# Loading one piece of a weight by three transfers of 112, 8 and 8 partitions instead of one of 128

## The chip, the cores and the metric

The kernel runs on one core of a Trainium2 chip. The time is that of one launch on the device, in microseconds (us); the figure for a kernel is the median of several runs. A profile is one execution of the same program recorded by the hardware profiler. It tells the time of every instruction, and it tells of the core's 16 DMA engines how many packets and bytes they moved, and when.

## What is computed

One decoding step of a transformer block: attention over a cache of 4,096 keys and values for each of 4 sequences and 32 heads, beside a small network, all in float32.

```python
x = A_x
xn = _layernorm(x, axis=-1)
return x + _A_ref(xn, A_k_cache, A_v_cache, A_wq, A_wo) + _B_ref(xn, B_w1, B_w2, B_w3, B_w4)
```

`_A_ref` is the attention. Its last step is the output projection, a product with the weight `wo` of 4,096 rows and 512 columns (8 MB):

```python
q = (x @ wq).reshape(B, Sq, H, Dh).transpose(0, 2, 1, 3)
scores = jnp.einsum("bhqd,bhkd->bhqk", q, k_cache) * (Dh ** -0.5)
p = _softmax(scores, axis=-1)
o = jnp.einsum("bhqk,bhkd->bhqd", p, v_cache)
return o.transpose(0, 2, 1, 3).reshape(B, Sq, H * Dh) @ wo
```

With one position for each sequence the shifts of `_B_ref` bring in nothing but zeros, so of that network `w3` and `w4` alone are read.

## The kernel before

The two caches are 2 x 256 MB. The kernel walks over 32 groups of four heads of one sequence (`NJ`), and for each group it loads 8 MB of keys into one of two buffers `ks`, and 8 MB of values into the buffer `vs`. VectorE multiplies the keys with the query and sums (lines 329 and 330), ScalarE takes the exponentials (348), TensorE multiplies them with the values (382). All loads are issued from one queue, SP, in the order of the program, each as soon as its buffer is free.

The end of the program is what the change touches. When VectorE has used the last keys (`SUMMED[LAST]`), SP loads `wo` into the buffer `ks` that is then free. Partition p holds 32 rows of `wo` (`WC`), one behind the other, 2 KB each. The loading is cut by rows of each partition, `wo_cuts`: 16, 8, 4, 2 and 1 rows; the last row follows in two halves of 256 columns (lines 290 to 292). Each of the seven pieces has a semaphore of its own, `wo_sems[n]`, that its transfer raises by 16.

TensorE takes the pieces in the same order (lines 414 to 434) and waits before each for its semaphore. It multiplies the rows of the first two pieces into four partial results in the bank `y`, and those of the others into the bank `total`; behind the piece of four rows (24 to 27) it adds the partial results to `total` through ScalarE's copy `ys` and the matrix `sel`. Behind each half of the last row the result is copied out of `total` by VectorE and ScalarE (436, 437) and stored by a DMA of four partitions (441). The four partitions are the four sequences.

Of the kernel before, what the change touches and what calls it, by code (L numbers as in the profile page):

```python
# [44 lines left out]
P = 128  # L45
# [4 lines left out]
PE, DVE, ACT = mybir.EngineType.PE, mybir.EngineType.DVE, mybir.EngineType.Activation  # L50
# [38 lines left out]
def decode_block(ctx: ExitStack, tc: tile.TileContext, x, k, v, wq, wo, w3, w4, out):  # L89
    nc = tc.nc  # L90
# [57 lines left out]
    def blocks4(start, stop, w, m, src):  # L148

        for t in range(4):  # L150
            i = nc.tensor.matmul(total[32 * t:32 * t + m, :], w, src[:, P * t:P * t + P], start=start, stop=stop)  # L151
        return i

    do = Steps(nc)
# [4 lines left out]
    wo_sb = ks[LAST % 2].rearrange("p (c n) -> p c n", c=WC)  # L159
# [125 lines left out]
    do.wait("SP", [SUMMED[LAST]])  # L285
    wo_r = wo.rearrange("(p c) n -> p c n", c=WC)
    for (c0, c1), sem in zip(wo_cuts, wo_sems):
        nc.sync.dma_start(wo_sb[:, c0:c1], wo_r[:, c0:c1]).then_inc(sem, 16)  # L288
    half = D // 2
    for n, sem in enumerate(wo_sems[-2:]):  # L290
        n *= half
# [120 lines left out]
    ys = os.rearrange("p m d -> p (m d)")  # L412
    do.wait("PE", [X_ok])
    for (c0, c1), sem in zip(wo_cuts, wo_sems):
        do.wait("PE", [(sem, 16)])
        for c in range(c0, c1):
            if c < 24:
                t = (c + 2) % 4
                i = nc.tensor.matmul(y[32 * t:32 * t + B, :], X[:, c, :], wo_sb[:, c], start=False, stop=(c >= 20))
            else:  # L420
                i = blocks4(False, False, X[:, c, :], B, wo_sb[:, c])
        d = do("PE", lambda e: i)

        if c1 == 24:
            ys_ok = do("ACT", lambda e: e.copy(ys, y), d)
        elif c1 == 28:
            do.wait("PE", [ys_ok])
            blocks4(False, False, sel, 32, ys)
# [49 lines left out]
```

## Time and profile before

| | us |
|---|---|
| median of 3 runs | 1302.82 |
| lowest and highest run | 1302.47, 1303.36 |
| span of the profiled execution, first to last instruction | 1301.2 |
| TensorE busy | 370.9 |
| VectorE busy | 1164.4 |
| ScalarE busy | 93.6 |

The difference between the median and the span, 1.6 us, lies around the instructions that the profile counts. VectorE is busy for 89% of the span. The share of the DMA engines is in the next section, with the rows that belong to it. A DMA is shown twice: as the instruction of the engine that issues it (SPq, ACTq), which is short, and as the packets that the 16 DMA engines move afterwards; the time "to landing" runs from the issue to the last increment of its semaphore.

### The profile page before, as it was taken

The page shows a single profiled execution, that of the slowest core. Times are in us where ns is not written, and L with a number is a line of the kernel's source. Part 1 is how long each engine was busy: PE and PEld are TensorE (multiplying, and loading weights), DVE is VectorE, ACT ScalarE, POOL GpSimd, SP SyncE. Part 2 cuts the span into 40 slices and gives each one's busy share as a digit, 9 for nine tenths or more (in the row PEclk, how much of TensorE's full clock was granted, in tenths as well). Part 3 has the DMA queues.
Part 4 walks back from the last instruction along what each step waited for, and adds up shares of the span by engine and source line. Part 5 has one row for each costly group of instructions (what it writes and reads, how often), then busy time and mean ns, then how long its engine had stood idle before and what let it go on. Part 6 is the DMA issues. An engine that isn't in the chain of part 4 may idle for free. (4 is left out here: it accounts for less than half of the span.)

```text
span 1301.2 us, 6686 instructions
## 1 busy us (share of the span) xinstructions
PE 370.9 (29%) x2652; PEld 132.4 (10%) x2652; DVE 1164.4 (89%) x323; ACT 93.6 (7%) x332; POOL 2.5 (0%) x14
## 2 busy tenths in 40 slices
PE   3221233321233321233331133332123332123338
PEld 1000111100011110011110011110001110001112
DVE  3499999999999999999999999999999999999990
ACT  1000000000000000000000000000000000000001
POOL 0000000000000000000000000000000000000000
PEclk9655666655666665666665666665666665566668
DMA  9999999999999999999999999999999999999998
GB/s 404 446 422 448 425 441 427 433 435 425 445 423 445 425 443 425 433 435 427 443 423 445 425 443 427 435 433 429 439 423 447 423 443 427 439 429 433 435 423 372
DMA packets 10830, 561.08 MB, mean 431 GB/s; under 512 B 1212, under 2 KB 1476, under 8 KB 1736
## 3 DMA queue, kind: packets, MB, share of 16 engines
q1 hardware_dynamic: 10808, 561.00, 99.7%
q8 instruction: 3, 0.05, 0.0%
q14 instruction: 3, 0.02, 0.0%
q10 hardware_dynamic: 16, 0.01, 0.0%
HBM read 561.00 MB, written 0.01 MB: 431 GB/s over the span
## 5 line engine op out<-in xcount | busy, mean ns | idle before, releaser
L329 DVE TENSOR_TENSOR ks<-ks,qb 128x8192 f32<-128x8192 f32 x64 | 556.3, 8692 | 59.2 <-DVEq L297 54.2
L330 DVE TENSOR_REDUCE sc<-ks 128x64 f32<-128x8192 f32 x64 | 555.9, 8686 | 2.2
L382 PE MATMUL pv<-vs,pw 128*32 128x512 f32 x1984 | 285.6, 740 | 869.7 <-PEq L297 869.7
L382 PEld LDWEIGHTS pv<-vs,pw 128*32 128x32 f32 x1984 | 78.5, 133 | 1052.2 <-issue 1052.2
L353 ACT COPY os<-pv 128x512 f32<-128x512 f32 x32 | 18.8, 586 | 827.7 <-ACTq L297 827.7
L348 ACT ACTIVATE pw<-sc,small 32x128 f32<-32x128 f32 x128 | 50.9, 398 | 275.2 <-ACTq L297 274.0
L387 PE MATMUL poz<-sel,os 128*128 128x4 f32 x256 | 32.8, 252 | 28.0 <-PEq L297 28.0
L387 PEld LDWEIGHTS poz<-sel,os 128*128 128x128 f32 x256 | 31.0, 191 | 56.1 <-issue 56.1
L348 ACT ACTIVATION_READ_ACCUMULATOR pw<-sc,small 32x1 f32 x128 | 23.5, 184 | 0.0
L436 DVE COPY os<-total 4x128 f32<-4x128 f32 x2 | 0.6, 282 | 15.0 <-PE total L434 15.0
L335 DVE TENSOR_REDUCE small<-sc 128x1 f32<-128x128 f32 x32 | 9.2, 286 | 4.7
L363 DVE RECIPROCAL rz<-oz 128x96 f32<-128x96 f32 (+1 forms) x2 | 1.1, 553 | 13.6 <-ACT oz L355 13.5
L389 PE MATMUL poz<-rs,ones 128*128 128x4 f32 x64 | 11.7, 253 | 0.0
L321 DVE STREAM_TRANSPOSE qb<-qg 128x128 f32<-128x128 f32 x32 | 10.0, 311 | 1.1
L264 DVE STREAM_TRANSPOSE vs<-pw 128x1024 f32<-128x1024 f32 x1 | 1.2, 1245 | 10.4 <-ACT pw L263 10.4
L320 DVE COPY qg<-qT 128x4 f32 x32 | 5.4, 170 | 5.1 <-issue 4.7
L389 PEld LDWEIGHTS poz<-rs,ones 128*128 128x128 f32 x64 | 9.7, 192 | 0.0
L382 PE MATMUL pv<-ks,pw 128*32 128x512 f32 x64 | 9.5, 757 | 0.0
L202 DVE TENSOR_REDUCE lns<-vs 4x1 f32<-4x512 f32 x1 | 0.7, 674 | 9.5 <-DMA vs<-in_A_x_dram 9.5
L355 ACT COPY oz<-poz 128x8 f32 x32 | 5.3, 166 | 50.8 <-ACTq L297 50.8
L215 PE MATMUL pt<-vs,pw 4*128 4x4 f32 x16 | 4.0, 372 | 16.4 <-DVE pw L209 16.4
L336 DVE STREAM_TRANSPOSE tr<-small 128x32 f32<-128x32 f32 x32 | 6.8, 212 | 1.1
(75 smaller groups left out, 78.4 us busy)
## 6 DMA issues: line engine op xcount, KB each, us to landing
ks<-in_A_k_cache_dram SPq DMA_DIRECT2D x2, 4096.0 KB, 26.9
vs<-in_B_w_dram SPq DMA_DIRECT2D x2, 3584.0 KB, 14.1
ks<-in_A_wo_dram SPq DMA_DIRECT2D x1, 4096.0 KB, 21.8
ks<-in_A_wo_dram SPq DMA_DIRECT2D x1, 2048.0 KB, 26.3
ks<-in_A_wo_dram SPq DMA_DIRECT2D x1, 1024.0 KB, 28.3
ks<-in_A_wo_dram SPq DMA_DIRECT2D x1, 512.0 KB, 29.1
ks<-in_A_k_cache_dram SPq DMA_DIRECT2D x31, 42.2
vs<-in_A_v_cache_dram SPq DMA_DIRECT2D x31, 26.8
```

The source lines that it names most:

```text
L320: step(e.tensor_copy(qg, pairs[:, s, bass.ds(j, 1)].rearrange("p o n -> p (o n)")))
L321: step(e.transpose(qb.rearrange("p (n m) -> p n m", m=HP), qg.unsqueeze(2).to_broadcast([P, DH // HP, HP])))
L329: step(e.tensor_tensor(out=kt, in0=kt, in1=qb.unsqueeze(1).to_broadcast([P, w, DH]), op=ALU.mult))
L330: step(e.reduce_sum(sc[s][:, c:c + w], kt, axis=AX.X))
L335: step(e.reduce_max(rm, sc[s], axis=AX.X))
L336: step(e.transpose(tr[s], rm.to_broadcast([P, HP])))
L348: i = nc.scalar.activation(pw[hp, :, 4 * h:4 * h + 4], sc[s][hp, :].rearrange("p (g w) -> p g w", w=4), AF.Exp, bias=small[hp, s, 1:2], sc ...
L353: nc.scalar.copy(os, pv.rearrange("p (m d) -> p m d", m=4)).then_inc(sems["copied"], 1)
L355: nc.scalar.copy(ozs[:, s, :, bass.ds(j, 1)].rearrange("p n o h -> p n (o h)"), poz[:, 0:2 * G].rearrange("p (n h) -> p n h", n=2)).then_i ...
L382: i = nc.tensor.matmul(pv[32 * t:32 * t + 32, :], pw[:, g, :], vt[:, 4 * g:4 * g + 4, :], start=(g < 4), stop=(g >= NG - 4))
L387: nc.tensor.matmul(poz[:, 0:G], os[:, m, :], sel.rearrange("p (h m) -> p m h", m=4)[:, m, 0:G], start=(m == 0), stop=(m == 3))
L389: nc.tensor.matmul(poz[:, G:2 * G], ones.to_broadcast([P, P]), rs, start=True, stop=True).then_inc(sems["poz"], 1)
```

## The change

The piece of rows 24 to 27 of each partition (1 MB, 8 KB on each partition) is loaded by three transfers: one for the partitions 0 to 111, one for 112 to 119, one for 120 to 127. All three raise the same semaphore, and TensorE waits for 48 instead of 16. The same bytes go to the same places, and the other six pieces are loaded as before.

```diff
     for (c0, c1), sem in zip(wo_cuts, wo_sems):
-        nc.sync.dma_start(wo_sb[:, c0:c1], wo_r[:, c0:c1]).then_inc(sem, 16)
+        for p0, p1 in ((0, 112), (112, 120), (120, P)) if c0 == 24 else ((0, P),):
+            nc.sync.dma_start(wo_sb[p0:p1, c0:c1], wo_r[p0:p1, c0:c1]).then_inc(sem, 16)
...
     for (c0, c1), sem in zip(wo_cuts, wo_sems):
-        do.wait("PE", [(sem, 16)])
+        do.wait("PE", [(sem, 48 if c0 == 24 else 16)])
```

On SP's queue, at the end of the program, the loads of `wo` (`ks` is the buffer, `in_A_wo_dram` the weight in memory; the numbers are partitions x elements) stood before as follows:

```order
L288 DMA ks<-in_A_wo_dram 128x8192
L288 DMA ks<-in_A_wo_dram 128x4096
L288 DMA ks<-in_A_wo_dram 128x2048
L288 DMA ks<-in_A_wo_dram 128x1024
L288 DMA ks<-in_A_wo_dram 128x512
L292 DMA ks<-in_A_wo_dram 128x256 x2
L441 DMA out_dram<-os 4x256
```

and now, with all line numbers one higher:

```order
L289 DMA ks<-in_A_wo_dram 128x8192
L289 DMA ks<-in_A_wo_dram 128x4096
L289 DMA ks<-in_A_wo_dram 112x2048
L289 DMA ks<-in_A_wo_dram 8x2048 x2
L289 DMA ks<-in_A_wo_dram 128x1024
L289 DMA ks<-in_A_wo_dram 128x512
L293 DMA ks<-in_A_wo_dram 128x256 x2
L442 DMA out_dram<-os 4x256
```

Two issues more stand ahead of the last four pieces, which move back by two places. The instructions of the other engines keep their order and their number.

## The prediction

> **What bounds the kernel now.** I read the head of the page, the DMA part and the table of queues first, then the chain that ended last, then the last 6 us by the timeline and by short windows.
>
> ```profile
> span 1301.2 us, 6686 instructions
> DMA  9999999999999999999999999999999999999998
> DMA packets 10830, 561.08 MB, mean 431 GB/s; under 512 B 1212, under 2 KB 1476, under 8 KB 1736
> q1 hardware_dynamic: 10808, 561.00, 99.7%
> q8 instruction: 3, 0.05, 0.0%
> ```
>
> The 16 DMA engines are busy from the first slice to the last (nines, and 99.7% in SP's queue q1). What decides the time is the bytes and how evenly the engines carry them. One engine moves 561.00 MB / (16 x 0.997 x 1301.2 us) = 27.0 GB/s, so **8 KB take it 0.303 us**, and the piece of 1 MB, eight such rows on each engine, 2.42 us. The chain says the same of the end:
>
> ```profile
> 1268.12 28.33 DMA ks<-in_A_wo_dram
> 1296.45 0.04 issue
> 1296.49 1.27 PE total L151 x40
> 1297.77 0.01 issue
> 1297.78 1.02 PE total L151 x24
> 1298.80 0.70 PE total L434 x8
> 1299.50 0.02 issue
> 1299.52 0.26 ACT os L437
> ```
>
> The DMA in the first row is the piece that the change cuts. It is issued at 1268.12, lies in the queue behind other loads, and lands at 1296.45; TensorE starts on it 0.04 us later. From there the chain looks like TensorE's, but the timeline of its weight loads shows that every later piece is waited for too:
>
> ```profile
> 1297.78 0.33 PEld L151 LDWEIGHTS total<-ks,X 128*4 128x4 f32 x16 [0.28 <-DMA ks<-in_A_wo_dram]
> 1298.39 0.11 PEld L151 LDWEIGHTS total<-ks,X 128*4 128x4 f32 x8 [0.29 <-DMA ks<-in_A_wo_dram]
> 1298.74 0.10 PEld L434 LDWEIGHTS total<-ks,X 128*4 128x4 f32 x4 [0.23 <-DMA ks<-in_A_wo_dram]
> 1299.06 0.10 PEld L434 LDWEIGHTS total<-ks,X 128*4 128x4 f32 x4 [0.23 <-DMA ks<-in_A_wo_dram]
> ```
>
> In brackets stands the idle time ahead of the row and what ended it. The end therefore moves with the landing of the last half row, just before 1299.06, nearly one to one.
>
> A transfer lands when its slowest engine is done. Windows at the end show how unequal the engines are (us, TensorE's granted clock, share of the 16 DMA engines by the packets that start in the window, GB/s):
>
> ```profile
> 1296.80:1297.20 0.40, 1.00 0.94 328
> 1297.20:1297.60 0.40, 1.00 0.60 210
> 1297.60:1297.90 0.30, 1.00 0.33 120
> 1297.90:1298.20 0.30, 1.00 0.27 96
> 1298.20:1298.50 0.30, 1.00 0.21 72
> 1298.50:1298.80 0.30, 1.00 0.04 14
> ```
>
> Nearly all 16 work until about 1297.1; then they run out one by one. From 1297.9 to 1298.2 some four are left (0.27 x 16 = 4.3), after 1298.2 about three (0.21 x 16 = 3.4), and these carry the end, some 1.6 us behind the first. One source of the lateness is in the trace. The three packets of q8 are fetches of instructions; a window around the last of them reads:
>
> ```profile
> DMA packets 5, 0.07 MB, mean 655 GB/s; under 512 B 0, under 2 KB 0, under 8 KB 0
> q1 hardware_dynamic: 4, 0.05, 115.2%
> q8 instruction: 1, 0.02, 67.9%
> ```
>
> 67.9% of 16 engines x 0.1 us (1292.8 to 1292.9) is 1.09 us on one engine, which so falls behind by as much. Nothing makes up for it later, because no engine ever runs empty and each transfer gives all engines the same.
>
> **The change, part by part.** *Two issues more on SP.*
>
> ```profile
> 1267.27 2.50 SPq L288 DMA_DIRECT2D ks<-in_A_wo_dram  x5
> 1269.82 0.90 SPq L292 DMA_DIRECT2D ks<-in_A_wo_dram  x2
> ks<-in_A_wo_dram SPq DMA_DIRECT2D x2, 128.0 KB, 28.8
> ```
>
> An issue takes about 0.45 us (0.90 / 2), so the four pieces behind are issued 0.9 us later, the last ones near 1271.2. They wait some 28.8 us in the queue today; 0.9 of it hides behind the loads ahead of them. Without that cover it would cost 0.9. Nothing else on SP is near: the store follows at 1299.5. Cost 0.
>
> *The wait for 48.* It replaces the wait for 16 in front of the same matmul, so TensorE gets no instruction more. The same matmuls stand behind it (rows 28 to 31 and both halves), and the copies and stores behind those. Cost 0, apart from a later landing.
>
> *The engines' rows.* Here lies the effect. How many engines a transfer uses can be counted from its closing packets: 75 loads of 128 partitions and three transfers of four partitions (x and two stores) make 75 x 16 + 3 x 4 = 1212 packets, exactly the page's "under 512 B 1212" (and q1's 10808 packets are 75 x (128 + 16) and 8 for one store). So 128 partitions close on 16 engines and four partitions on four, one each. The trace has no transfer of 112 or of 8. Bounds for 112: seven rows on each of 16 engines, or eight on each of 14; I take seven, nearer to the 128. Bounds for 8: all rows on one engine, or one on each of eight; I take eight, nearer to the four. Whether both small transfers use the same eight engines the trace doesn't show: if they use different ones, every engine has eight rows as today and nothing changes; if the same, eight engines get 7 + 1 + 1 = 9 rows and eight get 7. The three transfers of four partitions give no engine's name; I take the same, as two equal requests. Then **eight engines end 0.303 us later than today, eight 0.303 us earlier**.
>
> ```profile
> q1 hardware_dynamic: 8, 0.00, 1.0%
> q10 hardware_dynamic: 8, 0.00, 1.0%
> ```
>
> Closing packets add little. In the window 1299.8 to 1301.2, above, the two stores' 16 packets take 2.0% of 16 x 1.4 us, 28 ns each with the data among them, so two more are under 0.06 us. [...]
>
> *Sum.* The last landing is that of the latest engine. If at least one of the last three is among the eight with nine rows, the end moves by +0.303 us; if all four late ones are among the others, by up to -0.303. The trace names no engine. Taken at random, the four all fall into one given half in (8 x 7 x 6 x 5) / (16 x 15 x 14 x 13) = 4% of cases, the last three in (8 x 7 x 6) / (16 x 15 x 14) = 10%; so one of the latest is likely burdened, and I take +0.303. TensorE's idle 0.23 to 0.29 us could absorb nothing of a later landing. Against the profiled execution: span 1301.2 + 0.3 = 1301.5 us; the 1.6 us around it stay, so from the median 1302.82 the forecast is **1303.1 us**.
>
> **The rivals.** *The late engines are relieved.* If those that the fetches hit have seven rows, they gain 0.303 us; the next latest then decides. With three relieved and the fourth burdened it about cancels, since by the windows the fourth is done some 0.3 us before the three. This gives -0.3 to 0, 1302.5 to 1302.8. For it: the last three may have a common cause, the three packets of q8, and so may sit together. The case that nothing changes, because the two small transfers use different engines, falls here too.
>
> *The small transfers get in each other's way.* A transfer of 128 partitions spreads its writes over the whole memory on chip; eight neighbouring partitions are a sixteenth of it. If such a group takes no more than its share of the rate, 431 GB/s / 16 = 27 GB/s, its 64 KB need 2.42 us; with two shares 1.21 us; without a limit 0.303. One share costs 2 x (2.42 - 0.303) + 0.3 = +4.5 us, two 2 x (1.21 - 0.303) + 0.3 = +2.1: 1304.9. I take two shares as the bound of this case, between the ends, and think one share unlikely (3%). Part would hide, as the engines come to these rows up to 1.6 us apart: half of the 1.8 gives +1.2, 1304.0. Against it stands nothing in the trace: the transfers of four partitions are too small to show a rate. [...]
>
> *The small transfers aren't spread* (the one that ends slower by more than can be told from no change). If a transfer of eight partitions went to a single engine, both to the same, that engine would have 7 + 16 = 23 rows instead of eight, 15 x 0.303 = +4.5 us: 1307.4. It decides as soon as more than 2.6 / 0.303 = 8.6 extra rows fall on a late engine, so with one engine, not with two (seven extra rows, +2.1). Against it: four partitions close on four engines.
>
> **How the numbers follow.** Forecast 45% (1303.1, its own range 1302.8 to 1303.6, as the runs before lie 0.35 below to 0.54 above their median); late engines relieved or nothing changed 20% (1302.5 to 1302.8); in each other's way 25% (1303.4 to 1304.9), with one share 3% (1307.4); not spread 4% (1307.4); anything unseen 3%. The range for 8 in 10 reaches from 1302.3 (a relieved engine less some scatter) to 1304.9 (the bound of the third case). A measurement of this kernel can tell 0.2%, 2.6 us, from no change. More than that is lost only if the small transfers aren't spread or share one sixteenth of the rate: 7%. More than 2.6 us can't be won, as the whole lateness of the engines is 1.6 us: 1%, for the unseen. Within: 92%.
>
> **What would show it.** In the profile after: closing packets, 8 + 8 more under 512 B (1228) if each small transfer uses eight engines, 1214 if one; the last matmuls of the last half row starting 0.3 us later against the landing of the piece before; windows at the end with about as many late engines as now. A landing of the cut piece that is later by 1 us or more, with the DMA share staying high near 1296, speaks for getting in each other's way; by 4 us for one engine. I am wrong if the end moves by over 0.6 us either way, or if it moves while the cut piece lands when it does now.

## The result: 4 us slower, outside the range, and the profile after

| | before | after |
|---|---|---|
| median | 1303.01 us (1302.47 to 1303.41, 7 runs) | 1307.20 us (1306.25 to 1307.83, 7 runs) |
| span of the profiled execution | 1301.2 us | 1305.5 us |

The ratio is 1.0032, with a 95% interval of 1.0021 to 1.0042. The forecast was 1303.1 us, with a range up to 1304.9.

The DMA part of the page after has 16 more closing packets, and the same bytes:

```profile
span 1305.5 us, 6688 instructions
DMA packets 10846, 561.08 MB, mean 430 GB/s; under 512 B 1228, under 2 KB 1492, under 8 KB 1752
```

1228 is what the prediction gave for eight engines in each small transfer (1212 before). The chain that ended last, after:

```profile
1269.45 30.61 DMA ks<-in_A_wo_dram
1300.06 0.04 issue
1300.11 3.03 PE total L151 x64
1303.13 0.44 PE total L435 x8
1303.58 0.26 DVE os L437
```

The cut piece lands at 1300.06, 3.6 us later than before (1296.45). The last matmul ends at 1303.57 (1303.13 + 0.44) instead of 1299.50, 4.1 us later. Where the time went is shown by windows over the end. Before (us, TensorE's granted clock, share of the 16 DMA engines, GB/s):

```profile
1290.00:1292.00 2.00, 1.00 0.99 422
1292.00:1294.00 2.00, 1.00 0.98 397
1294.00:1296.00 2.00, 1.00 0.95 387
1296.00:1298.00 2.00, 1.00 0.79 287
1298.00:1300.00 2.00, 1.00 0.07 23
```

and after:

```profile
1290.00:1292.00 2.00, 1.00 0.98 414
1292.00:1294.00 2.00, 1.00 0.99 250
1294.00:1296.00 2.00, 1.00 1.04 252
1296.00:1298.00 2.00, 1.00 1.07 178
1298.00:1300.00 2.00, 1.00 0.90 200
1300.00:1302.00 2.00, 0.69 0.59 214
1302.00:1304.00 2.00, 0.50 0.00 0
```

Look at the last two columns together. From 1292 on the engines are as busy as before, and move 250 instead of 400 GB/s, then 178. They have the same packets in hand for longer, and the trace keeps the time of every packet. The piece is 128 packets of 8 KB in both kernels; half of them took at most 0.31 us before and 0.54 us after (the medians). The first of them starts at 1291.8 before and 1291.9 after; after the change the first three still take 0.31 us, and those that start from 1292.4 on take 0.5 us and more for the most part. So the loss begins when the first engines reach the transfer of 112 partitions, about 2 us (seven rows) before the small ones can be next. It holds up even a transfer that the change doesn't touch. The piece of eight rows ahead landed 26.3 us after its issue before:

```profile
ks<-in_A_wo_dram SPq DMA_DIRECT2D x1, 2048.0 KB, 26.3
```

and lands after 27.6 us now (the other rows are those of the last two halves and of SP's issues):

```profile
ks<-in_A_wo_dram SPq DMA_DIRECT2D x1, 2048.0 KB, 27.6
ks<-in_A_wo_dram SPq DMA_DIRECT2D x2, 128.0 KB, 31.3
1267.34 3.28 SPq L289 DMA_DIRECT2D ks<-in_A_wo_dram  x7
1270.66 0.90 SPq L293 DMA_DIRECT2D ks<-in_A_wo_dram  x2
```

The last half row lands 31.3 us after an issue that is 0.84 us later (1270.66 against 1269.82): 31.3 + 0.84 - 28.8 = 3.3 us later than before. The other 0.7 us up to the end of the matmuls goes with TensorE's granted clock, 0.69 and 0.50 in the last two windows, where it was 1.00 before. From 1300.11 on TensorE waits for no further piece; it is still at work on the earlier ones when the last half row lands.

### The profile page after: what moved, and what is told of

Its sections match the earlier page's. It is cut to its first block, busy times and chain, and to the rows that moved or that the text cites. A ratio compares the mean times of both kernels' runs of the same rounds, so it can differ in the third digit from the quotient of the medians.

```text
span 1305.5 us, 6688 instructions
## 1 busy us (share of the span) xinstructions
PE 367.9 (28%) x2652; PEld 132.6 (10%) x2652; DVE 1164.5 (89%) x323; ACT 93.5 (7%) x332; POOL 2.5 (0%) x14
## 2 busy tenths in 40 slices
DMA packets 10846, 561.08 MB, mean 430 GB/s; under 512 B 1228, under 2 KB 1492, under 8 KB 1752
## 5 line engine op out<-in xcount | busy, mean ns | idle before, releaser
L383 PE MATMUL pv<-vs,pw 128*32 128x512 f32 x1984 | 282.5, 733 | 873.0 <-PEq L298 873.0
## 6 DMA issues: line engine op xcount, KB each, us to landing
ks<-in_A_wo_dram SPq DMA_DIRECT2D x1, 2048.0 KB, 27.6
ks<-in_A_wo_dram SPq DMA_DIRECT2D x1, 512.0 KB, 31.3
```

What stands on the lines that cost most here:

```text
L383: i = nc.tensor.matmul(pv[32 * t:32 * t + 32, :], pw[:, g, :], vt[:, 4 * g:4 * g + 4, :], start=(g < 4), stop=(g >= NG - 4))
```

## The experiments

The theory after this, called **places**, is an assumption, no trace shows it: the memory on chip is made up of places that take no more than about one engine's rate each, 27 GB/s by the prediction. A transfer of 128 partitions would give every engine a place of its own; other transfers would let several engines write one place at once, and all of them would be slowed. Rivals: **small transfers alone** (only those of eight partitions cost), **rows** (only nine rows against seven), **source** (reading neighbouring rows is slow), and the plain number of transfers. In the diffs `...` is the unchanged load of the kernel before. TensorE waits for 16 times the number of transfers that stand for the piece or behind it, so 16, 32 or 48; the diffs leave that line out. Each time is a median; the ratio behind it, with its 95% interval, compares all runs with runs of the kernel before made beside them, and isn't the plain quotient of the medians.

### Two transfers of 112 and 16 partitions

```diff
-        for p0, p1 in ((0, 112), (112, 120), (120, P)) if c0 == 24 else ((0, P),):
+        for p0, p1 in ((0, 112), (112, 128)) if c0 == 24 else ((0, P),):
```

> The piece of four rows is loaded by two transfers, of partitions 0 to 111 and 112 to 127, so there is no transfer of eight partitions, and each engine should get 7 + 1 = 8 rows as before. [...] Rival 'small transfers alone' (the 112 is innocent, only transfers of eight partitions cost): 1303.0 to 1303.5. Rival 'rows' (only 9 rows against 7 on an engine count): 1303.0.

Measured: 1306.58 us, ratio 1.0029 (1.0018 to 1.0041), as slow as the changed kernel; the piece lands at 1300.28, 3.8 us later than before. The page counts 1228 closing packets, 76 x 16 + 3 x 4, so both transfers use 16 engines. No transfer of eight partitions and no engine with nine rows is needed for the loss: "rows" and "small transfers alone" fall.

### Two halves

```diff
+        for p0, p1 in ((0, 64), (64, 128)) if c0 == 24 else ((0, P),):
```

> The piece of four rows is loaded by two transfers, of partitions 0 to 63 and 64 to 127, four rows on each engine in each. 'Places': each half reaches half of the sixteenths, so two engines share one, until the first are done with a half and go on to the other; the piece lands 0.5 to 2.5 us later, 1303.5 to 1305.5 us, with the DMA share near 1 and fewer GB/s. 'Rows' and 'small transfers alone': 1303.0, no loss.

Measured: 1308.46 us, 1.0041 (1.0027 to 1.0055), 3 us above the range that "places" gave. The windows 1292 to 1296 and 1296 to 1300 of this run:

```profile
1292.00:1296.00 4.00, 1.00 1.03 223
1296.00:1300.00 4.00, 0.57 0.98 230
```

Full share and little more than half the rate (392 GB/s before, from 1292 to 1296), without any odd number of partitions. The theory's direction holds, its size was too small: the piece lands at 1301.10, 4.7 us later than before instead of 0.5 to 2.5. Why halves lose that much isn't shown.

### Additional small transfers, packed and spread

In both kernels the piece is one transfer of 128 partitions again, and two transfers of eight rows, which nobody uses, stand behind it. They differ only in where they write: packed, each transfer goes to eight neighbouring partitions; spread, to eight partitions four apart (0, 4, ... 28 and 1, 5, ... 29). "Places" assumes of the spread ones that each engine then writes to another place; no run shows that.

```diff
...
+        if c0 == 24:
+            for p0 in (112, 120):
+                nc.sync.dma_start(vs[p0:p0 + 8, 8192:10240], wo_r[p0:p0 + 8, c0:c1]).then_inc(sem, 16)
```

> The piece of four rows is one transfer of 128 partitions, as before. Behind it stand two more transfers of 8 KB from each of the partitions' rows 112 to 119 and 120 to 127, which nobody uses, into eight neighbouring partitions each of a part of vs that is free; TensorE waits for them too. Their bytes alone cost eight engines two rows, 2 x 0.303 = 0.6 us: 'rows' gives 1303.6. 'Places': eight engines share two sixteenths, twice 1.2 us: 1304.5 to 1306. 'Source' (it is the reading of neighbouring rows that is slow, not the writing): the same, 1304.5 to 1306.

```diff
+            for i, p0 in enumerate((112, 120)):
+                nc.sync.dma_start(vs[i:i + 32:4, 8192:10240], wo_r[p0:p0 + 8, c0:c1]).then_inc(sem, 16)
```

> [...] 'Places': no collision is left, only the bytes, 1303.3 to 1303.9 us, at least 1 us less than e3. 'Source': the same time as e3, 1304.5 to 1306. 'Rows': 1303.6, and e3 the same.

Measured: packed 1304.58 us, 1.0015 (1.0006 to 1.0025); spread 1302.77 us, 1.0002 (0.9992 to 1.0011). The windows 1294 to 1298, packed and then spread:

```profile
1294.00:1298.00 4.00, 0.95 1.00 261
```

```profile
1294.00:1298.00 4.00, 1.00 0.94 368
```

The same rows of `wo`, the same closing packets (1228), the same bytes (561.21 MB): the reading is not at fault, so "source" falls for these transfers. It is where they are written. The spread case is below its forecast of 1303.3 to 1303.9: not even its bytes cost anything that can be measured.

### Which destinations cost

Three more kernels change only the destination of the same two transfers: 16 partitions apart over the whole memory; four apart as in the free case, but 64 partitions higher; and packed, but at the low end.

```diff
+                nc.sync.dma_start(vs[i:i + 113:16, 8192:10240], wo_r[p0:p0 + 8, c0:c1]).then_inc(sem, 16)
```

> As e3 and e4 (two additional transfers of eight partitions behind the piece), but written to partitions 16 apart: 0, 16, ... 112 and 1, 17, ... 113. If a place is a block of eight neighbouring partitions, all eight rows have places of their own, and the time is that of e4, 1302.8 us. [...]

```diff
+                nc.sync.dma_start(vs[64 + i:64 + i + 29:4, 8192:10240], wo_r[p0:p0 + 8, c0:c1]).then_inc(sem, 16)
```

> As e4 (two additional transfers of eight partitions, written to partitions four apart), but into partitions 64 to 92 and 65 to 93 instead of 0 to 29. Engines and bytes are the same. If only engines count, or if all places are alike: 1302.8 as e4. 'Places', with the late engines' places among partitions 64 to 127: the rows stand in front of places that are still busy and end last, the last half row lands 0.3 to 0.7 us later than in e4: 1303.1 to 1303.6.

```diff
+            for q0, p0 in ((0, 112), (8, 120)):
+                nc.sync.dma_start(vs[q0:q0 + 8, 8192:10240], wo_r[p0:p0 + 8, c0:c1]).then_inc(sem, 16)
```

> As e3 (two additional transfers of eight neighbouring partitions behind the piece), but into partitions 0 to 7 and 8 to 15 instead of 112 to 127. All slow cases so far (e3, e8, e10) wrote at least half of their rows to partitions from 64 on, the one that cost nothing (e4) only below 32. 'Packing' (eight engines on two places share their rate, wherever these are): the last half row lands 0.5 to 1.5 us later than in e4 (1299.2), 1303.3 to 1304.5 us. 'Only the upper half' (rows in places of late engines cost, packing as such doesn't): as e4, landing at 1299.0 to 1299.4, 1302.8 to 1303.1 us.

The times: 1304.62 us, 1.0014 (1.0004 to 1.0023); 1304.55 us, 1.0013 (1.0004 to 1.0023); 1304.08 us, 1.0012 (1.0003 to 1.0021). The time can't tell these from each other or from the packed case; all of them are slower than the spread case. The start of the last weight load follows the last landing, and shows it in one execution of each. In this order: spread (free), 64 higher, packed low, 16 apart, packed at 112:

```profile
1299.22 0.10 PEld L437 LDWEIGHTS total<-ks,X 128*4 128x4 f32 x4 [0.19 <-DMA ks<-in_A_wo_dram]
```

```profile
1300.31 0.10 PEld L437 LDWEIGHTS total<-ks,X 128*4 128x4 f32 x4 [0.22 <-DMA ks<-in_A_wo_dram]
```

```profile
1300.36 0.10 PEld L437 LDWEIGHTS total<-ks,X 128*4 128x4 f32 x4 [0.22 <-DMA ks<-in_A_wo_dram]
```

```profile
1300.38 0.10 PEld L437 LDWEIGHTS total<-ks,X 128*4 128x4 f32 x4 [0.22 <-DMA ks<-in_A_wo_dram]
```

```profile
1300.93 0.10 PEld L437 LDWEIGHTS total<-ks,X 128*4 128x4 f32 x4 [0.19 <-DMA ks<-in_A_wo_dram]
```

Only one destination of five is free. Spreading isn't enough by itself (64 higher: 1.1 us later), and a low address isn't either (packed low: 1.1 us later, as "packing" had it; "only the upper half" falls). For "64 higher" I had expected a landing 0.3 to 0.7 us later and up to 1303.6 us; both are more. "16 apart" isn't free (1304.62 us, where blocks of eight gave 1302.8), which speaks against a place being a block of eight neighbouring partitions. That it lands before packed at 112 shows nothing by itself: packed low lands as early, and these are single executions. Why that one destination is free isn't shown: which engine writes which row would decide it by the theory, and the profile gives no engine's number.

### The transfer of 112 partitions by itself

First as an addition behind the whole piece, beside one of the same bytes that covers all partitions:

```diff
+        if c0 == 24:
+            nc.sync.dma_start(vs[:112, 8192:10240], wo_r[:112, c0:c1]).then_inc(sem, 16)
```

> The piece of four rows is one transfer of 128 partitions, as before. Behind it stands one more transfer of 8 KB from each of the partitions 0 to 111 (917 KB, seven rows on each engine), which nobody uses, into the free part of vs. Its bytes cost 7 x 0.303 = 2.1 us in any case: 1304.9. 'Places' (a transfer of 112 partitions is dealt so that engines collide, while one of 128 isn't): 1.5 to 3.5 us more than e6, 1306.5 to 1308.5. 'Small transfers alone': the same as e6, 1304.9.

```diff
+            nc.sync.dma_start(vs[:, 8192:9984], wo_r[:, c0:c1].rearrange("p c n -> p (c n)")[:, :1792]).then_inc(sem, 16)
```

> As e5, but the additional transfer carries the same 917 KB as 7 KB of each of 128 partitions. Every theory: bytes alone, 2.1 us more than the kernel before, 1304.9 us; the DMA engines go on at 400 GB/s and more.

Measured: 1309.06 us, 1.0048 (1.0031 to 1.0065), against 1305.45 us, 1.0020 (1.0010 to 1.0029). The windows 1295 to 1299, 112 partitions and then 128:

```profile
1295.00:1299.00 4.00, 0.97 0.99 244
```

```profile
1295.00:1299.00 4.00, 1.00 1.00 402
```

917 KB cost 2.6 us over 128 partitions (2.1 by the bytes) and 6.2 us over 112; both are above their forecasts, 1309.06 against at most 1308.5 and 1305.45 against 1304.9. The rows of the chain that show the additional transfer, 112 partitions and then 128, are

```profile
1268.67 32.74 DMA vs<-in_A_wo_dram
```

```profile
1268.48 30.36 DMA vs<-in_A_wo_dram
```

It lands at 1301.41 and 1298.84, so 2.6 of the 3.6 us between the two kernels are its landing. The rest goes with TensorE's matmuls behind it, which ran at a granted clock of 0.50 from the start in the first kernel and for the later part in the second. Then as a part of the changed kernel, with the two small transfers left out:

```diff
+        p1 = 112 if c0 == 24 else P
+        nc.sync.dma_start(wo_sb[:p1, c0:c1], wo_r[:p1, c0:c1]).then_inc(sem, 16)
```

> The changed kernel without its two transfers of eight partitions: the rows of partitions 112 to 127 in the piece of four rows are not loaded (128 KB of 1 MB are left out, and the product uses what lies there). Each engine has seven rows instead of eight, 0.3 us less than the kernel before if nothing collides: 1302.5 ('small transfers alone'). 'Places': the 112 by itself is slowed to some 250 GB/s, 917 KB take 3.7 instead of 2.1 us: 1304 to 1305.5.

Measured: 1305.42 us, 1.0020 (1.0011 to 1.0030), within the range that "places" gave: 2.5 of the 4.2 us, though an eighth of the piece's bytes is missing. The windows 1292 to 1296 and 1296 to 1300, and the last weight load:

```profile
1292.00:1296.00 4.00, 0.95 1.01 242
1296.00:1300.00 4.00, 1.00 0.94 254
```

```profile
1301.60 0.10 PEld L435 LDWEIGHTS total<-ks,X 128*4 128x4 f32 x4 [0.22 <-DMA ks<-in_A_wo_dram]
```

The rate falls as in the changed kernel (251 GB/s from 1292 to 1296) without any small transfer; at 242 GB/s over 16 engines 8 KB take one engine 0.54 us, as the packets there. The last weight load starts 2.5 us later than before (1299.06), so all of the 2.5 us is landing. The other 1.8 us come with the small transfers, but not all by the DMA: the last half row lands 3.3 us late in the changed kernel, 0.8 more than here, and 0.7 us there goes with the low clock, which is 1.00 here.

For the transfer of 112 partitions no run varied the destination as for the small ones. That its rows are slow is shown; that it is because engines write one place at once is the theory, and a slower reading of these rows isn't ruled out for it.

### The number of transfers

```diff
+        for p0, p1 in ((0, 1792), (1792, 1920), (1920, 2048)) if c0 == 24 else ((0, (c1 - c0) * D),):
+            nc.sync.dma_start(wo_sb[:, c0:c1].rearrange("p c n -> p (c n)")[:, p0:p1],
+                              wo_r[:, c0:c1].rearrange("p c n -> p (c n)")[:, p0:p1]).then_inc(sem, 16)
```

> The piece of four rows is loaded by three transfers of 917, 64 and 64 KB, as in the changed kernel, but cut along the rows: all three are of 128 partitions (1,792, 128 and 128 columns of each). TensorE waits for 48. 'Places': nothing collides, 1302.8 to 1303.3 us. If it were the number of transfers, the two more issues on SP or the wait for 48 that cost: 1306 to 1307, as the changed kernel.

Measured: 1302.99 us, 1.0000 (0.9991 to 1.0010). Three transfers, two more issues and a wait for 48 cost nothing that can be measured, if each covers all partitions.

### The changed kernel again

> The changed kernel itself, a second profile. 'Places': the DMA share stays near 1 with 150 to 280 GB/s from 1292 to 1300, and the last half row lands 3 us or more later than before (1302 to 1302.6), as in the first profile. Open is the granted clock of TensorE at the end, 0.50 in the first profile: if it is part of the loss, it is 0.50 again; if it is a matter of when TensorE's slow stretches happen to fall, it may be 1.00, and the last matmul then ends within 0.6 us of the last landing, not 1.2.

Measured: 1307.64 us in one run, beside 1302.79 in one run of the kernel before. The end of the chain, and the window 1302 to 1304:

```profile
1300.44 0.04 issue
1300.48 3.58 PE total L151 x64
1304.06 0.28 PE total L435 x8
```

```profile
1302.00:1304.00 2.00, 0.51 0.01 4
```

The landing is as late, and the clock low again. In the kernel with the 112 alone the same matmuls ran at 1.00, and its last matmul ended 0.44 us after the last weight load had begun. The first weight load behind the piece tells the profiles apart. In the changed kernel (first profile), and then in the kernel with the 112 alone:

```profile
1300.11 0.82 PEld L151 LDWEIGHTS total<-ks,X 128*4 128x4 f32 x32 [3.77 <-DMA ks<-in_A_wo_dram]
```

```profile
1299.24 0.77 PEld L151 LDWEIGHTS total<-ks,X 128*4 128x4 f32 x32 [2.81 <-DMA ks<-in_A_wo_dram]
```

In the two profiles of the changed kernel the weight loads had been idle here for 3.77 and 3.72 us, and the clock fell to 0.50 for the matmuls behind it. In seven profiles in which it stayed at 1.00 (the kernel before, the 112 alone, and the additional small transfers) they had been idle for 1.42 to 2.81 us. With the additional transfer of 128 partitions the clock fell too (0.50 from 1300 to 1302), so slow packets aren't needed for it. In these nine a long wait goes with the low clock, then, but no run changed the wait alone, and whether the wait brings it or the place of TensorE's slow stretches in time stays open. It is worth 0.7 of 4.1 us in the first profile.

## Why the prediction was wrong

- **The step that failed** is "the engines' rows". It spread the 112 partitions over 16 engines, as the closing packets confirm (152 from 1260 us on in the kernel with the 112 alone, as many as before), and priced each row at 0.303 us as in a transfer of 128. That price was right for the piece before the cut (0.31 us a packet), and wrong for the transfer of 112, where the same 8 KB took 0.54 us. The engines then move some 250 GB/s in place of 400, and this part alone is 2.5 us. By the theory the price holds only where each engine writes a place of its own; for the 112 this last step is not shown.
- **The rival "in each other's way"** stood at 25%, and its sign came: the cut piece landed 3.6 us later with the DMA share near 1 at 1296. Its price for the two small transfers, +1.2 to +2.1 us, is about what they cost when packed behind the whole piece: 1.8 us at partitions 112 to 127, 1.1 at 0 to 15. Its bound was added up from two shares of the rate for eight partitions, which no run shows; the runs show only that the time depends on where the rows are written (1302.77 us spread, 1304.58 packed). What it left out is the big transfer, the other 2.5 us, and so the total lies beyond its bound. The total came near the 1307.4 us of two other cases, but by luck and not by their mechanisms: the small transfers use eight engines each (1228 closing packets), and the packed ones cost far less than the 4.5 us of one share.
- **Late engines.** The +0.3 us of the forecast rested on one of the latest engines getting nine rows. The spread case, which puts two rows more on eight engines if both transfers use the same ones, shows no measurable cost, its last weight load 0.16 us later (1299.22 against 1299.06) and not 0.6. That speaks for the latest three being among the other eight, as the rival of the relieved engines had it, but the profile names no engine. It is one execution each, and nothing came of it here.
- **SP's two issues, the wait for 48**: nothing that can be measured, as forecast; the cut along the rows shows it.
- **The end moves with the landing**, nearly one to one: 3.3 of 4.1 us. The clock of the last matmuls was not foreseen.
- **Chances.** 7% stood for slower by over 0.2%. The interval, 0.21% to 0.42%, lies just above that bound.

## What to carry to other kernels

Where DMA engines set the time, as at the end of this kernel, cut a transfer along the free dimension (the elements within a partition) and leave it at all 128 partitions: the three-way cut along rows cost nothing that could be measured, the one along partitions 4 us on 1 MB. In a profile the sign is a DMA share near 1 with fewer GB/s than elsewhere (here 250 and less instead of 400): each packet of 8 KB then takes longer, 0.54 us instead of 0.31. To count the rows of each engine isn't enough. It also matters where the rows are written: the same two small transfers cost nothing at one destination and 1.1 to 1.8 us at the four others.

## What the runs showed of the hardware that was not expected

Two equal halves of 64 partitions are no better than the uneven cut: 1308.46 us, at 223 to 230 GB/s, against 1307.20, though the intervals of the two ratios overlap. And a transfer can slow one that stands ahead of it in the same queue: the untouched piece of eight rows landed 1.3 us later (27.6 against 26.3 us from its issue). By the theory, early engines would already have been writing the next transfer to places where late ones still wrote; the profile shows the delay, not the places.
